# Loading half of one V unit of layer two by seven row-strided transfers instead of as part of one whole transfer

## The chip, the core and the metric

The kernel runs on one core of one Trainium2 chip. The metric is the time of one execution on the device in microseconds (us). Three runs of the kernel before took 648.73, 648.85 and 649.52 us; their median is 648.85 us. One further execution was recorded by the hardware profiler; all durations below are from it.

## What is computed

Two layers, each an attention block over a cache and a small gated network, applied twice to four rows `x` (one new token for each of four sequences). Both passes read the same weights and caches.

```python
def _A_ref(x, k_cache, v_cache, wq, wo):          # x (4,1,512), caches (4,8,8192,128) bf16
    q = (x @ wq).reshape(B, 1, 32, 128)           # 32 query heads, 8 cache heads
    scores = einsum("bhqd,bhkd->bhqk", q, k) * Dh ** -0.5
    o = einsum("bhqk,bhkd->bhqd", softmax(scores), v)
    return o.reshape(B, 1, 4096) @ wo
def _B_ref(x, w_gate, w_up, w_down):              # F = 1792
    return (silu(x @ w_gate) * (x @ w_up)) @ w_down
x = x + _A_ref(_layernorm(x), ...)
x = x + _B_ref(_layernorm(x), ...)
x = x + _A_ref(_layernorm(x), ...)
x = x + _B_ref(_layernorm(x), ...)
```

K and V together are 128 MiB, and each layer reads nearly all of it, so the work is mostly transfers from HBM into the on-chip memory (SBUF, 128 partitions).

## The kernel before, in words

**Units.** K and V are cut into 16 units each: two cache heads of one sequence. A unit fills one slot of the tile `kvf`, 128 partitions with 32 KB each. Partition p holds 128 consecutive tokens of one of the two heads, so the row that goes to a partition is one contiguous stretch of 32 KB in HBM. A unit is used in eight column blocks of 4 KB per partition (`NB = 8`, `BW` elements each); half a unit is 16 KB per partition.

**What is done with a unit.** For a K unit VectorE transposes each block in place (`turn`, line 488), TensorE multiplies each with the query (`scores`, line 512), then come the maximum, the exponentials on ScalarE (line 559) and the turning of the probabilities (line 576). For a V unit TensorE multiplies the probabilities with it in four parts (`values`, line 643; the first two parts read the first half), and VectorE gathers the result (lines 689 and 693). At the end of a layer the heads are mixed and projected (lines 724 to 784), and `ffn` runs the gated network (lines 876 and 897, with the weights loaded into a slot that has come free).

**Slots and loads.** There are four slots and a fifth (`QS`), and about 273 MB pass through them. All loads are issued by the SyncE queue (SP), in one order written out beforehand: the list `cmds` (lines 346 to 364). Layer two takes its units in the order 15, 14, 13, 12, 0 to 11; `loads` interleaves K and V, and `placed` deals them to the slots of a ring and cuts some into pieces (`half`, `ends`). A load enters the program when the column blocks it overwrites have been used: `freed` marks blocks as free and calls `pump`, which appends the next loads of the list as long as their blocks are free. On the chip the SP instruction then waits for the semaphore of the engine that used the block last (TensorE, for the units below). Because all five slots are kept full, SP is about three units ahead: a load is issued 30 to 40 us before it has landed.

**The unit of the change** is V of unit 5, the tenth in layer two's order (`V(1, us[9])`; "V9" below). It goes into slot 0 after K of unit 4 has been used there. In the profile SP issues it at 490.23 us, between K of the eleventh unit (472.97 us, "K10") and the next K ("K11", 492.40 us).

**Completion.** A transfer adds 16 to its semaphore when it has landed; the 16 DMA engines of the core share it. `load` (line 424) issues exactly one transfer for each entry of `cmds`.

Of the kernel before, what the change touches and what calls it, by code (L numbers as in the profile page):

```python
# [103 lines left out]
def bass_interleave_layers__gqa_block_cached__swiglu_ffn__decode_kernel(  # L104
# [18 lines left out]
    P = 128  # L123
# [6 lines left out]
    NB = 8  # L130
# [14 lines left out]
    with ExitStack() as es:  # L145
# [3 lines left out]
        BW = TB * Dh  # L149
# [6 lines left out]
        kv = kvf[:, 0:(NSLOT + 1) * SL].rearrange("p (s w) -> p s w", s=NSLOT + 1)  # L156
# [126 lines left out]
        T = _Sync(engines, prog)  # L283
# [35 lines left out]
        def pair_gb(u):  # L319
            return u // B, u % B  # L320

        order = [list(range(NP)), [NP - 1, NP - 2, NP - 3, NP - 4] + list(range(NP - 4))]
# [3 lines left out]
        V = lambda L, u: ("V", L, u)  # L326

        def loads(L, first):
            us = order[L]
            seq = []  # L330
            for i in range(first, NP - 1):
                seq += [K(L, us[i]), V(L, us[i - 1])]
            seq.insert(len(seq) - 1, K(L, us[NP - 1]))
            return seq[:-2] + [seq[-2], seq[-1], V(L, us[NP - 2]), V(L, us[NP - 1])]

        ends = lambda it, s: [(it, s, 0, QH), (it, s, QH, NB - 1), (it, s, NB - 1, NB)]
        half = lambda it, s: [(it, s, q, q + NB // 2) for q in range(0, NB, NB // 2)]

        def placed(seq, ring, parts):
            out = []  # L340
            for i, it in enumerate(seq):
                s = ring[i % len(ring)]
                out += parts[i](it, s) if i in parts else [(it, s, 0, NB)]
            return out

        us = order[0]
        seq = [K(0, us[0])] + loads(0, 1)
        assert len(seq) == 2 * NP
        cmds = placed(seq, (0, 1, 2, 3), {len(seq) - 1: ends})
# [6 lines left out]
        us = order[1]  # L356
        s = W_SLOT[0]
        cmds += [(K(1, us[1]), s, 0, 3), (K(1, us[1]), s, 3, 4), (K(1, us[1]), s, 4, NB)]
        cmds += [(K(1, us[2]), QS, 0, NB // 2), (K(1, us[2]), QS, NB // 2, NB - 2)]
        seq = loads(1, 3)  # L360
        ring = (0, 1, 3, QS, 2)
        cmds += placed(seq, ring, {0: half, 1: half, len(seq) - 1: ends})
        assert W_SLOT[1] == ring[len(seq) % len(ring)]
        cmds += [(("W", 1), W_SLOT[1], 0, NB), (("W+", 1), W_SLOT[1], NB, NB + 1)]

# [39 lines left out]
        def pump():  # L405
            while issued[0] < len(cmds):
                it, s, a, b = cmds[issued[0]]
                if it[0] == "wo":
                    load_weight(*it)
                else:  # L410
                    need = {(s, q) for q in range(a, b)}
                    if not need <= free:
                        return
                    free.difference_update(need)
                    if it[0] in ("W", "W+"):
                        load_weight(it[0], it[1], s)
                    else:
                        slot_of[it] = s
                        load(it, a, b, sem_s[s] if b - a == NB else part_sem())
                issued[0] += 1  # L420

        q_gone = set()

        def load(it, a, b, sm):
            kind, L, u = it
            s = slot_of[it]
            gp, bt = pair_gb(u)
            src = (A_k_cache if kind == "K" else A_v_cache)[bt, 2 * gp:2 * gp + 2, :, :].rearrange(
                "h (p t) d -> (h p) (t d)", t=TT)
            over = WQ if s == QS and not q_gone else []  # L430
            q_gone.update(over)
            T.dma("sp", kv[:, s, a * BW:b * BW], src[:, a * BW:b * BW], sm,
                  writes=[f"s{s}.{q}" for q in range(a, b)] + over)

        def freed(s, a, b):
            free.update((s, q) for q in range(a, b))
# [492 lines left out]
        for L in range(2):  # L929
            us = order[L]  # L930
# [61 lines left out]
```

## Time and profile before

| what | value |
|---|---|
| median of three runs | 648.85 us |
| the profiled execution's own time | 648.29 us |
| its span, first to last instruction | 646.50 us |
| bytes moved, mean rate over the span | 273.37 MB, 423 GB/s |
| V9 issued / landed | 490.23 / 525.17 us |
| last V pieces landed | 628.73, 632.46, 633.73 us |
| last weight piece (`w_down`) landed | 643.81 us |
| output issued | 644.94 us |

The profile's page lists busy time of each engine (PE is TensorE's matmul, PEld its weight loads, DVE VectorE, ACT ScalarE, POOL GpSimd, SP SyncE), then digits for 40 slices of the span (9 is 90% busy or more), the DMA queues, and the chain of work that ended last: from the last instruction back, each time to what released it. Besides these views the trace keeps, for every transfer, the times at which its semaphore was raised by each DMA engine (the landing records), and, for every DMA packet, its start, length and size (the packet records). Packet records do not name their engine, but on one engine a packet starts within a few nanoseconds of the end of the one before it, so the 16 series of packets can be followed from start to end.

### The profile page before, as it was taken

To read this page: it belongs to the slowest core of one execution; us is meant where nothing else is said; L and a number is where in the kernel's file an instruction comes from. 1 tells how busy PE (TensorE), PEld (TensorE's weight loads), DVE (VectorE), ACT (ScalarE), POOL (GpSimd) and SP (SyncE) were. 2 spreads that over 40 slices of the span, in tenths; PEclk is the share of its full clock that TensorE was granted. 3 is DMA by queue.
4 is the path that set the end of the run, shared out by engine and by line. 5 is a ranking of instruction groups with operands and counts; after the bars stand their busy time and mean duration, and the time that the engine had idled before them with its cause. 6 is when DMAs were issued, how large, how long until landed. Compare 5 with 4: busy or idle time off the path is not lost.

```text
span 646.5 us, 7503 instructions
## 1 busy us (share of the span) xinstructions
PE 425.6 (66%) x3128; PEld 173.1 (27%) x3128; DVE 430.1 (67%) x706; ACT 41.2 (6%) x117; POOL 11.1 (2%) x43
## 2 busy tenths in 40 slices
PE   2574466556766755767757987777665576657878
PEld 2221122212322212222226332222222222222225
DVE  1585467566776666777852878888766677766953
ACT  1000000000000000001010010000000000000110
POOL 0000000000000000000000000000000000000000
PEclk9996896789787999878985799999878997789977
DMA  9999999999999999999999999999999999999996
GB/s 363 445 423 416 442 429 430 426 435 433 426 430 435 430 425 436 435 422 436 434 407 409 396 435 434 434 429 423 442 427 426 433 438 424 431 440 423 430 417 268
DMA packets 14129, 273.37 MB, mean 423 GB/s; under 512 B 1416, under 2 KB 1424, under 8 KB 5264
## 3 DMA queue, kind: packets, MB, share of 16 engines
q1 hardware_dynamic: 14096, 272.91, 99.0%
q8 instruction: 24, 0.39, 0.2%
q14 instruction: 9, 0.07, 0.0%
HBM read 272.90 MB, written 0.00 MB: 422 GB/s over the span
## 4 chain that ended last, share of the span: by engine, by line
DMA 61%; DVE 26%; PE 9%; issue 3%; SPq 0%; ACT 0%; DVEq 0%
DMA kvf<-in_A_k_cache_dram 49%; DVE kvf L488 20%; DMA kvf<-in_A_v_cache_dram 10%; PE ps L512 3%; DVE pT L576 3%; PE ps L643 2%; DMA kvf<-in_B_w_down_dram 2%; DVE pb L693 2%; PE ps L839 1%; DVE pb L689 0%; PE ps L876 0%; DVE scr L703 0%; DVE kvf L452 0%; PE ps L759 0%; SPq L93 0%
## 5 line engine op out<-in xcount | busy, mean ns | idle before, releaser
L512 PE MATMUL ps<-kvf,zq 128*128 128x512 bf16 x1024 | 298.0, 426 | 181.1 <-DVE kvf L488 174.3
L488 DVE STREAM_TRANSPOSE kvf<-kvf 128x1024 f32<-128x1024 f32 x246 | 289.8, 1219 | 108.6 <-DMA kvf<-in_A_k_cache_dram 107.7
L512 PEld LDWEIGHTS ps<-kvf,zq 128*128 128x128 bf16 x1024 | 90.6, 105 | 350.9 <-DVE kvf L488 257.8
L643 PE MATMUL ps<-kvf,pT 128*32 128x512 bf16 x960 | 66.7, 400 | 1.4 <-DVE pT L576 0.8
L559 ACT ACTIVATE pb<-ps,tiny 128x512 bf16<-128x512 f32 x32 | 22.0, 688 | 531.8 <-DVE tiny L557 495.2
L576 DVE STREAM_TRANSPOSE pT<-pb 64x512 bf16<-64x512 bf16 x60 | 41.2, 687 | 3.1 <-ACT pb L559 2.0
L518 DVE TENSOR_REDUCE tiny<-ps 128x1 f32<-128x512 f32 x32 | 22.0, 687 | 31.6 <-PE ps L512 31.6
L693 DVE SCALAR_TENSOR_TENSOR pb<-ps,tiny,pb 128x128 f32<-128x128 f32 x104 | 36.5, 351 | 5.1 <-PE ps L643 1.3
L643 PEld LDWEIGHTS ps<-kvf,pT 128*32 128x32 bf16 x960 | 20.8, 98 | 31.9 <-issue 15.7
L698 PEld LDWEIGHTS ps<-sel,pb 128*128 128x128 f32 x64 | 15.4, 258 | 21.3 <-DVE pb L693 14.0
L502 POOL TENSOR_TENSOR zq<-scr,tiny 128x64 bf16<-128x64 bf16 x30 | 9.0, 300 | 564.8 <-PE ps L512 564.8
L526 DVE TENSOR_REDUCE mrm<-ps 1x8 f32<-1x128 f32 x32 | 8.8, 275 | 14.2 <-PE ps L523 14.2
L698 PE MATMUL ps<-sel,pb 128*128 128x8 f32 x64 | 12.7, 272 | 8.1 <-DVE pb L693 8.1
L549 PEld LDWEIGHTS ps<-mrm,tiny 128*128 128x128 f32 x60 | 12.0, 205 | 8.6 <-DVE scr L703 3.2
L759 PE MATMUL ps<-wo_sb,scr 128*4 128x512 bf16 x48 | 11.0, 379 | 1.5 <-DVE scr L728 1.5
L689 DVE TENSOR_SCALAR pb<-ps,tiny 128x128 f32<-128x128 f32 x32 | 10.1, 315 | 2.6 <-PE ps L643 2.6
L549 PE MATMUL ps<-mrm,tiny 128*128 128x16 f32 x60 | 9.3, 231 | 3.1 <-ACT mrm L561 3.1
L839 PE MATMUL ps<-xn,kvf 128*128 128x4 bf16 x256 | 7.6, 166 | 3.8 <-DMA kvf<-in_A_wq_dram 3.0
L561 ACT ACTIVATE mrm<-head,tiny 128x8 f32<-128x8 f32 x32 | 9.6, 301 | 1.0
L523 PE MATMUL ps<-identf,tiny 128*1 128x128 f32 x32 | 8.6, 270 | 0.2 <-DVE tiny L518 0.2
L839 PEld LDWEIGHTS ps<-xn,kvf 128*128 128x128 bf16 x256 | 7.6, 106 | 4.0 <-DMA kvf<-in_A_wq_dram 3.1
L876 PE MATMUL ps<-xn,kvf 128*128 128x4 bf16 x224 | 7.3, 169 | 1.8 <-DMA kvf<-in_B_w_up_dram 1.4
(83 smaller groups left out, 113.9 us busy)
## 6 DMA issues: line engine op xcount, KB each, us to landing
kvf<-in_A_k_cache_dram SPq DMA_DIRECT2D x28, 4096.0 KB, 30.8
kvf<-in_A_v_cache_dram SPq DMA_DIRECT2D x27, 4096.0 KB, 32.9
kvf<-in_A_v_cache_dram SPq DMA_DIRECT2D x4, 2048.0 KB, 20.0
kvf<-in_A_k_cache_dram SPq DMA_DIRECT2D x4, 2048.0 KB, 10.0
kvf<-in_A_wq_dram SPq DMA_DIRECT2D x2, 2048.0 KB, 9.8
wo_sb<-in_A_wo_dram SPq DMA_DIRECT2D x4, 1024.0 KB, 40.6
kvf<-in_B_w_gate_dram SPq DMA_DIRECT2D x2, 1792.0 KB, 24.5
kvf<-in_A_v_cache_dram SPq DMA_DIRECT2D x2, 1536.0 KB, 34.8
```

The costliest lines, as they stand in the source:

```text
L488: T.op("dve", lambda e: e.transpose(w, w), reads=[f"s{s}.{q}"], writes=[f"s{s}.{q}"])
L512: T.op("pe", lambda e: e.matmul(bank(bk)[:, 0:SW], lhsT=zq[:, z0:z0 + P], rhs=w[:, :, c // 2, :, c % 2], start=(q == 0 and c == 0), stop=( ...
L518: T.op("dve", lambda e: e.tensor_reduce(mx[:], bank(bk)[:, 0:SW], AX.X, ALU.max), reads=[f"pb{bk}"], writes=["mx"])
L549: T.op("pe", lambda e: e.matmul(at, lhsT=ones, rhs=mrm[:, i * H2:(i + 2) * H2], start=True, stop=True), reads=[f"m8{i}", "rsm", "onesf"], ...
L559: T.op("act", lambda e: e.activation(pb[:], bank(bk)[:, 0:SW], ACTF.Exp, bias=nm, accum_out=rs), reads=[f"pb{bk}", "nm"], writes=PB + ["rs"])
L576: T.op("dve", lambda e: e.transpose(dst, pb[hp]), reads=["pb", "row"], writes=[name])
L643: T.op("pe", lambda e: e.matmul(bank(k)[j * QB:(j + 1) * QB, q0 * Dh:q1 * Dh], lhsT=p_t[:, t, h, :], rhs=v[:, q0:q1, t, :], start=((last o ...
L689: T.op("dve", lambda e: e.tensor_scalar(into, o, own[:, q:q + 1], None, op0=ALU.mult), reads=[f"pb{k}", "own"], writes=["row"] if last els ...
L693: T.op("dve", lambda e: e.scalar_tensor_tensor(into, o, own[:, q:q + 1], into, op0=ALU.mult, op1=ALU.add), reads=[f"pb{k}", "own", iname], ...
L698: T.op("pe", lambda e: e.matmul(at, lhsT=into, rhs=sel[:], start=True, stop=True), reads=[iname, "sel"], writes=[name])
L759: T.op("pe", lambda e: e.matmul(bank(OUTB)[0:B, 0:D], lhsT=oT[:, h, :], rhs=wo_sb[:, h, :], start=(gp == groups[L][0] and r == 0), stop=(g ...
L839: T.op("pe", lambda e: e.matmul(at[:, h * B:(h + 1) * B], lhsT=wq_sb[:, kt, h * Dh:(h + 1) * Dh], rhs=xn[:, kt * B:(kt + 1) * B], start=(k ...
```

## The change

The list of loads cuts V9 into two halves, and the first half (columns 0 to 3 of 8, 16 KB in each partition) is issued as seven transfers over strided partitions: the 64 odd ones; the 32 that leave 2 when divided by 4; the 16 that leave 4 when divided by 8; and then four transfers of four partitions, 0, 32, 64, 96, and the same shifted by 8, 16 and 24. The seven share one semaphore, the second half has another. The wait for the slot is made once, ahead of the seven.

```diff
         seq = loads(1, 3)
         ring = (0, 1, 3, QS, 2)
-        cmds += placed(seq, ring, {0: half, 1: half, len(seq) - 1: ends})
+        cut = lambda it, s: [(it, s, 0, 4), (it, s, 4, NB)]
+        cmds += placed(seq, ring, {0: half, 1: half, seq.index(V(1, us[9])): cut, len(seq) - 1: ends})
...
+        uneven = (V(1, order[1][9]), 0)
+
         def load(it, a, b, sm):
...
-            T.dma("sp", kv[:, s, a * BW:b * BW], src[:, a * BW:b * BW], sm,
-                  writes=[f"s{s}.{q}" for q in range(a, b)] + over)
+            names = [f"s{s}.{q}" for q in range(a, b)] + over
+            rows = [slice(0, P)]
+            if (it, a) == uneven:
+                rows = [slice(i, P, m) for i, m in ((1, 2), (2, 4), (4, 8), (0, 32), (8, 32), (16, 32), (24, 32))]
+                T.wait_res("sp", writes=names)
+            for r in rows[:-1]:
+                T.dma("sp", kv[r, s, a * BW:b * BW], src[r, a * BW:b * BW], sm)
+            T.dma("sp", kv[rows[-1], s, a * BW:b * BW], src[rows[-1], a * BW:b * BW], sm, writes=names)
```

In the program that is built, the one SP entry of V9 becomes eight: 64, 32, 16 and four times 4 rows, and 128 rows for the second half. The order of the instructions of the other engines is the same.

## Prediction

> **What bounds the kernel now.** I began with the page: its span, the slices, and the DMA queues.
>
> ```profile
> span 646.5 us, 7503 instructions
> ...
> DMA  9999999999999999999999999999999999999996
> ...
> q1 hardware_dynamic: 14096, 272.91, 99.0%
> q8 instruction: 24, 0.39, 0.2%
> q14 instruction: 9, 0.07, 0.0%
> ```
>
> All 40 slices of the DMA row but the last are at 9, and the kernel's own loads (q1) fill 99.0% of the span of all 16 DMA engines. Queues 8 and 14 are instruction fetches: 24 of 16 KB and a few of 8 KB, which pass through the same engines. The busy time by stretch says the same of layer two: DMA share 1.00 and 1.01 up to 588 us, while TensorE and VectorE work two thirds of the time.
>
> ```profile
> 372.00:484.00 112.00, 80.70 (x510) 29.91 (x509) 86.34 (x135) 7.35 (x22) 2.10 (x7) 0.95 1.00 431
> 484.00:588.00 104.00, 66.13 (x393) 24.51 (x391) 71.75 (x108) 6.41 (x18) 1.80 (x6) 0.87 1.01 432
> 588.00:634.00 46.00, 35.20 (x241) 13.03 (x233) 32.13 (x60) 4.30 (x13) 0.79 (x2) 0.89 0.99 422
> ```
>
> Next the chain that ended last, in order of time.
>
> ```profile
> 472.97 42.49 DMA kvf<-in_A_k_cache_dram
> ...
> 588.37 40.36 DMA kvf<-in_A_v_cache_dram
> 628.73 0.04 issue
> 628.77 1.90 PE ps L643 x16
> ...
> 642.61 1.67 PE ps L897 x53
> 644.28 0.27 DVE pb L960
> ```
>
> It runs through long waits for transfers up to 628.73 us, then through the tail of the kernel. In the tail TensorE still waits for transfers: for the last two V pieces (landed 632.46 and 633.73 us, used at 632.50 and 633.78) and for the last weight piece, in the timeline of the end:
>
> ```profile
> 642.52 1.72 PE L897 MATMUL ps<-kvf,pb 128*4 128x128 bf16 x56
> 643.85 0.10 PEld L897 LDWEIGHTS ps<-kvf,pb 128*4 128x4 bf16 x8 [0.17 <-DMA kvf<-in_B_w_down_dram]
> ```
>
> So the end is the stream of transfers plus a fixed 2.7 us (643.81 to 646.50). What counts is when the **latest** DMA engine finishes, since a transfer has landed only when all its engines have. The landing records show how unequal they are: the first and last engine of V9 land 3.00 us apart (522.17 and 525.17), those of the last whole V unit 4.51 us apart (619.31 and 623.82), those of the last weight piece 4.33 us apart. Sorted, the engines' lags at that last V unit are 0, 0.13, 0.23, 0.70, 1.36, 1.42, 1.55, 1.69, then a step to 2.40, five from 2.77 to 2.92, 3.97 and 4.51 us. The packet records say why: each 16 KB instruction fetch puts the engine it falls on back by about 1.5 us. Eight engines are hit in turn, every eighth fetch the same one; after 370 us the other eight are spared. The spared are the first eight of the list.
>
> **The change, part by part.** *Rows per engine.* A whole transfer of 128 rows gives each engine 8 rows. The landing records show 16 raises for such a transfer, but for the one load of four rows (`x`, 1 KB each) four raises by engines and one more: four rows use four engines, one row each, and in the packet records four series hold one 1 KB packet each. I read the change by this: 64, 32 and 16 rows give every engine 4 + 2 + 1 = 7 rows, and the four transfers of four rows give 4 more to the same four engines. Twelve engines then carry 7 rows instead of 8 in this half, four carry 11. That all four-row transfers take the engines of `x` is my reading; the only other such load, the output, comes after a pause across which the series cannot be followed.
>
> *Price of a row.* Four half units in a row (issued 363.87 to 375.98 us) land at 374.51, 379.42, 384.30 and 389.21: 4.90 us for 8 rows of 16 KB, 0.612 a row. The six whole units that land from 515.47 to 573.75 us come every 9.71 us. A completion costs an engine one 4-byte packet of 9 ns in the packet records; I take 0.01 us.
> - Twelve engines: 7 x 0.612 + 3 x 0.01 + 4.90 (second half) = 9.21 us against 9.71: **0.50 us gained**.
> - Four engines: 11 x 0.612 + 7 x 0.01 + 4.90 = 11.70 us: **1.99 us lost**.
>
> *Which four.* Followed through the packet series from the 1 KB packets at 7.6 to 7.9 us, the four that loaded `x` are not among the eight hit by the 16 KB fetches up to 263 us; two of the four are followed clearly, two pass close to others. If so, their lag at the last V unit is at most 1.69, and 1.69 + 1.99 = 3.68 us, less than the 4.51 - 0.50 = 4.01 us of the latest. The latest engine gives 0.50 us and no other takes its place; the margin is 0.33 us. From there all remaining loads end 0.50 us earlier.
>
> *Is the 0.50 us passed on?* The loads behind V9 are queued long before, so every later landing moves by it. In the tail the V pieces, and the weight piece that ends last, are waited for by TensorE within 0.04 us of landing; the work between (633.78 to 642.52) follows from a landing as well and moves with it. So the whole is on the path: 0.50 us.
>
> *SP.* Seven issues more, 0.33 us each and 0.37 to 0.51 apart (606.80, 607.23, 607.74): up to 3.6 us. The first seven wait for the first four blocks of the K unit in slot 0 instead of all eight. In PE's timeline that unit's matmuls run from 477.92 us, the fourth block's end near 484 and the eighth's at 490.15; so the seven are out by 488, and the second half goes at 490.23 as V9 does now. Queued behind them on SP is K11 (492.40). Cover: at 484 us K10's load still has 31 us to go (landing 515.47). Without it each late issue would cost what it is late. I count nothing. Ten loads stood issued and not landed at 327 us, now twelve at 492; if the queue took no more, SP would stall a little inside the same cover.
>
> *Waits.* TensorE waits for V9 on two semaphores instead of one, once 0.05 us, in an engine with a third of its time free: nothing. The next load into the slot waits for both: landed long before.
>
> *Strided rows.* No transfer before has partitions in strides, so this cost is bounded. Below: zero, since a row of 16 KB takes 0.61 us in all loads. Above: each row at half the rate, 7 x 0.61 = 4.3 us on all engines. Nearest row: the four `x` packets go to partitions 0 to 3, two of them run at the same time (7.768 to 7.816 us), and all four take 46 ns; they do not slow each other. They are small, so I keep both ends and take zero.
>
> A rule against this: the Trainium skill, "SBUF — State Buffer", section "Door 1: The DMA port swizzle", says that groups of four partitions share a DMA port, 32 apart the same one. By it an engine that takes partitions 1, 3, 5, 7 changes port midway and meets another engine there, as far as ports are the limit; by it the sum could be the +3.8 us of the second rival. No run so far shows it.
>
> Sum: -0.50 us. On the profiled execution 648.29 - 0.50 = 647.8 us; it lies 0.56 us under the median, which gives 648.85 - 0.50 = **648.3 us** (0.08% less, within the 0.2%, or 1.3 us, that a measurement of this kernel can tell from no change).
>
> **Rivals.**
> 1. *The four engines are late ones.* For: two series are not certain. Against: the count above. From a lag of 4.01 - 1.99 = 2.02 us on they become the latest: with one of the group near 2.9 the end moves by 2.9 + 1.99 - 4.51 = +0.4, with the very latest by +2.0. 649.2 to 650.9 us.
> 2. *Slower: strided rows share ports.* Place: the seven transfers; price 0.61 us a row at half rate. It eats the gain from 0.07 us a row on (0.50 / 7), and shows as over 0.2% from 0.26 a row on (1.8 / 7). All seven rows: +4.3 - 0.5 = +3.8, 652.6 us; half of them, +1.6, 650.5 us. For: partitions never taken in this order before. Against: the `x` packets.
> 3. *It does not do what it says.* If the four-row transfers are spread over all 16 engines, each has 8 rows as now and pays some completions: +0.1, 648.9 us. Against: five raises for `x` instead of 16.
> 4. *More than 0.5 us.* A tail that answers more than one to one, down to 647.5 us. Nothing in the views shows where from; a gain over 0.61 us, one row, has no place in the sum.
>
> **How the numbers follow.** Forecast 0.62 (its own range 647.9 to 648.8, the scatter of the runs shown); rival 1 0.12; rival 2 0.14; rival 3 0.08; rival 4 0.04. The range 647.9 to 650.1 holds the forecast, rival 3 and most of rival 1, and leaves out most of rivals 2 and 4. Slower by over 0.2%: rival 2 and the worst of rival 1, 0.16. Faster by over 0.2%: 0.02. Within: 0.82.
>
> **What would show it.** In the profile after: 64 more semaphore packets and 128 more data packets on q1; the landing records of K11 and later 0.50 us earlier; first-to-last spreads 0.5 us smaller or led by other engines; the 2.7 us after the last weight piece as now. If the landing of the seven comes several us late, rival 2; if later spreads grow, rival 1; if nothing moves, rival 3. The forecast is wrong too if the fetches fall on other engines in other executions.

## The result, and the profile after

Six runs of the changed kernel took 654.02 to 656.21 us, median **655.22 us**; six of the kernel before 648.61 to 649.52, median 648.97. The ratio is 1.0096 (95% interval 1.0084 to 1.0107): 6.25 us slower, where 0.5 us less was forecast and 650.1 was the end of the range. The profiled execution took 654.25 us. One of the five executions of e10 below took 1940.22 us and is left out of its ratio.

From the page of the changed kernel, the span, the DMA digits, the rate by slice and the DMA queues:

```profile
span 652.5 us, 7511 instructions
...
DMA  9999999999999999999999999999999999999995
GB/s 368 433 425 420 440 431 428 429 434 429 430 432 429 432 431 434 431 430 430 426 411 401 416 437 429 436 425 435 428 431 432 353 406 436 427 434 431 428 415 207
...
q1 hardware_dynamic: 14288, 272.91, 98.7%
q8 instruction: 24, 0.39, 0.2%
q14 instruction: 9, 0.07, 0.0%
```

The bytes and the instruction fetches are those of before, q1 has 192 packets more (14,096 before), and the DMA digits are again all 9. By them nothing has changed. The rate row has the loss in two slices of 16.3 us: the 32nd and 33rd, 353 and 406 GB/s, from 506 to 538 us, around the landing of V9. Finer stretches show how deep it is. The next two answers are the busy times by stretch of the kernel before and then of the changed one, around the landing of V9; the last three columns are the granted TensorE clock, the share of time in which the DMA engines were busy, and GB/s.

```profile
509.00:515.00 6.00, 2.75 (x36) 0.84 (x34) 0.97 (x2) 0.00 (x0) 0.30 (x1) 1.00 1.01 434
515.00:521.00 6.00, 4.00 (x13) 1.67 (x14) 5.40 (x8) 0.00 (x0) 0.00 (x0) 0.72 1.01 431
521.00:527.00 6.00, 4.76 (x21) 1.60 (x19) 5.90 (x11) 1.08 (x3) 0.00 (x0) 1.00 0.96 415
527.00:533.00 6.00, 3.19 (x37) 1.05 (x37) 1.90 (x3) 0.00 (x0) 0.30 (x1) 1.00 0.99 426
```

```profile
509.00:515.00 6.00, 2.92 (x37) 0.90 (x35) 0.97 (x2) 0.00 (x0) 0.30 (x1) 1.00 0.96 410
515.00:521.00 6.00, 4.04 (x11) 1.74 (x12) 5.23 (x8) 0.00 (x0) 0.00 (x0) 0.56 1.09 287
521.00:527.00 6.00, 5.54 (x22) 2.15 (x20) 5.90 (x11) 1.08 (x3) 0.00 (x0) 0.87 0.97 322
527.00:533.00 6.00, 3.27 (x37) 1.05 (x37) 2.10 (x3) 0.00 (x0) 0.30 (x1) 1.00 1.03 442
```

From 515 to 527 us the busy share stays near 1 while the rate falls from 430 to about 300 GB/s: a packet that is held up counts as busy, so only bytes per time tell. The packet records say the same. Of the 256 packets of 16 KB of V9, 81 took over 1000 ns instead of 612, on all 16 engines, between 515.80 and 526.94 us; summed, 3.68 us more per engine. The 64 odd rows before them ran at 611 to 622 ns.

The landing records give the second part. K10 landed at 515.64 us (515.47 before), so everything up to there is as before. V9's first engine landed at 525.21 (522.17 before, +3.0), its last at 531.68 (525.17, +6.5); the spread from first to last grew from 3.0 to 6.5 us and stayed above 6 in the units behind. So some 3 us came to all engines and another 3 to one engine. K11 landed at 541.39 (534.90), the last weight piece at 649.79 (643.81). The chain and the end of the timeline show the delay passed on. The chain's wait for K11 is 48.84 us from issue to landing, against 42.50 before (492.40 to 534.90):

```profile
492.55 48.84 DMA kvf<-in_A_k_cache_dram
...
648.48 1.80 PE ps L906 x54
```

```profile
649.83 0.10 PEld L906 LDWEIGHTS ps<-kvf,pb 128*4 128x4 bf16 x8 [0.28 <-DMA kvf<-in_B_w_down_dram]
...
650.91 0.30 SPq L971 DMA_DIRECT2D out_dram<-pb  x1
```

The last product still waits for the last weight piece, and 2.7 us remain after its landing (649.79 to 652.5), as before.

### The profile page after: what moved, and what is told of

The parts are those of the page before. It is cut to its first block, busy times and chain, and to the rows that moved or that the text cites. A ratio compares the mean times of both kernels' runs of the same rounds, so it can differ in the third digit from the quotient of the medians.

```text
span 652.5 us, 7511 instructions
## 1 busy us (share of the span) xinstructions
PE 424.1 (65%) x3128; PEld 173.3 (27%) x3128; DVE 430.2 (66%) x706; ACT 41.2 (6%) x117; POOL 11.1 (2%) x43
## 4 chain that ended last, share of the span: by engine, by line
DMA 56%; DVE 30%; PE 9%; issue 3%; ACT 0%; SPq 0%; POOL 0%; ACTq 0%; POOLq 0%; DVEq 0%
DMA kvf<-in_A_k_cache_dram 50%; DVE kvf L497 22%; DMA kvf<-in_A_v_cache_dram 4%; PE ps L521 4%; DVE pT L585 3%; DVE pb L702 3%; PE ps L652 2%; DMA kvf<-in_B_w_down_dram 2%; DVE pb L698 1%; PE ps L848 1%; PE ps L885 0%; DVE scr L712 0%; DVE ps L464 0%; DVE tiny L527 0%; DVE kvf L461 0%
```

## Experiments

Most of these kernels change only the line `rows = [...]` of the changed kernel, so that its list is the whole diff. e5 and e6 also read from a second list, and e8 and e16 add transfers to the kernel before; of these four the main lines are shown. Each is compared with the kernel before on the same chip (648.36 to 648.48 us in the four groups). "Excess" is the time above 0.612 us of V9's 16 KB packets, summed and divided by 16 engines.

**Is it the cut, the unequal rows, the order or the strides?** The first group: the cut alone; equal rows with 16-row transfers; neighbouring partitions; and four-row transfers eight apart instead of 32.

```diff
e1  rows = [slice(0, P)]
e2  rows = [slice(i, P, m) for i, m in ((1, 2), (2, 4), (4, 8), (0, 8))]
e3  rows = [slice(i, i + n) for i, n in ((0, 64), (64, 32), (96, 16), (112, 4), (116, 4), (120, 4), (124, 4))]
e4  rows = [slice(i, P, m) for i, m in ((1, 2), (2, 4), (4, 8))] + [slice(i, i + 32, 8) for i in (0, 32, 64, 96)]
```

> V9 in two halves of 128 rows each, no seven transfers. All theories: the cut is not the cause; 649.0 us, within 0.3 us of before, packets of the half at 0.61 us. If it is over 650, the cut itself (its second semaphore or the earlier issue) has a share.

Measured 648.51 us, ratio 1.0001 [0.9991, 1.0010]; excess 0.07 us. The cut costs nothing.

> First half as 64, 32, 16 and 16 strided rows: 8 rows for each engine, no four-row transfers. Theory P (strided partitions contend, from the 16-row transfer on, for whatever they share): slower, two rows of eight at half rate or worse, 650 to 653 us, with packets of over 1 us. Theory F (the four-row transfers alone slow all engines): as before, 649.0 us. Theory I (only the unequal load of 11 rows): as before, 649.0.

Measured 651.80 us, 1.0051 [1.0036, 1.0066]; excess 2.49 us. The spread between the engines has not grown (2.2 us in V9's second half and behind it, 3.0 before). Every engine has its 8 rows here, so 3.4 us come from the way the rows are cut, without any inequality.

> The same seven sizes over neighbouring rows: 0 to 63, 64 to 95, 96 to 111, then 112 to 127 in fours. Theory P (stride): packets back at 0.61 us and only the unequal load left, 648.5 to 651. Theory F: slow packets as in the changed kernel, 654 to 656. If neighbouring rows contend more than strided ones (each small transfer then lies in few groups of partitions), over 656.

Measured 661.27 us, 1.0200 [1.0183, 1.0217]; median packet 1170 ns, excess 8.58 us, slow from 512.0 us on, so from the first transfer. The same numbers of rows in neighbouring partitions cost twice as much.

> 64, 32 and 16 rows as in the changed kernel; the four-row transfers take partitions 8 apart (0, 8, 16, 24 and so on) instead of 32 apart. If the four-row transfers contend because two of their four partitions lie 32 apart, 650 to 652 us with fewer slow packets; if it is the 16-row transfer or the unequal load, as the changed kernel, 654 to 656.

Measured 654.40 us, 1.0099 [1.0084, 1.0114]: as the changed kernel. How far the four rows stand apart hardly matters.

**HBM or SBUF?** A transfer's rows are strided on both sides. e5 keeps the SBUF partitions of the changed kernel and reads neighbouring rows of HBM; e6 does the reverse (partitions of e3, strided rows of HBM). e7 is 64 odd and 64 even partitions. e8 puts three tiny loads of one, two and four rows (8, 12 and 10 bytes) ahead of four V units of the kernel before; their sizes make them findable in the packet records, so that they tell when the engines that serve them get there.

```diff
e5, e6  T.dma("sp", kv[r, s, a * BW:b * BW], src[f, a * BW:b * BW], sm)   # f: the other order
e7      rows = [slice(i, P, 2) for i in (1, 0)]
e8      for n, w in ((1, 4), (2, 6), (4, 5)):
            T.dma("sp", mark[0:n, at_m[0]:at_m[0] + w], src[0:n, 0:w], m, writes=[f"mark{at_m[0]}"])
            at_m[0] += w
```

> The seven transfers with the strided partitions of the changed kernel, but each reads neighbouring rows from HBM, as in e3; so half a unit of V stands in other partitions than its own, and the output is not the reference's. If the contention lies on the SBUF side (which partitions are written together): as the changed kernel, 654 to 656 us, slow packets from about 515.8 us on, 3.7 us lost per engine. If it lies on the HBM side (which rows are read together): as e3, 660 to 662 us, 8.6 us lost per engine.

> The reverse of e5: neighbouring partitions are written as in e3, rows are read from HBM with the strides of the changed kernel; half a unit of V stands in other partitions than its own, and the output is not the reference's. SBUF side: as e3, 660 to 662 us, slow packets from 512 us on. HBM side: as the changed kernel, 654 to 656 us.

e5 654.72 us, 1.0096 [1.0075, 1.0116]; e6 661.42 us, 1.0199 [1.0179, 1.0219], two executions each. e5 is the changed kernel again, e6 is e3 again. The SBUF partitions decide, the rows of HBM do not.

> First half as two transfers of 64 rows, the odd partitions and the even ones: 8 rows for each engine. The 64-row transfer of the changed kernel ran at full rate in its packet records, so the theory that only the sparser strides (16 rows, every eighth partition) contend gives no change, 648.4 us within 0.5. If any stride contends once it is the last one out, over 650 us.

Measured 648.46 us, 1.0004 [0.9994, 1.0013], median packet 613 ns. Stride 2 is free.

> The kernel before, with three tiny transfers of one, two and four rows (8, 12 and 10 bytes a row) ahead of four of the loads, V9's among them; they go to a spare tile that nothing reads. Nothing is left out; time as before, within 0.5 us. The odd sizes show in the packet records which series belong to the engines that serve four-row transfers. Theory of the prediction: all four among the eight earliest at V9, lag under 1.8 us. Theory that the unequal load costs: at least one of the four among the late ones, near 2.9 us.

Measured 648.66 us, 1.0001 [0.9991, 1.0011]. The four packets of 10 bytes start at 512.42, 512.44, 513.03 and **515.53** us ahead of V9, and at 609.52, 609.56, 610.16 and 613.65 ahead of a later V unit. Of the four engines three are early and one is 3 to 4 us late, in the kernel before already. The loads of one and two rows ran on early ones.

**Which sets are slow?** Four more cuts of the half. With 112 rows and then fours or pairs the rows of each engine are 7 and 11 (or 15); with 32 and 16 rows they are 8 everywhere.

```diff
e9   rows = [slice(16, P)] + [slice(i, i + 4) for i in (0, 4, 8, 12)]
e10  rows = [slice(16, P)] + [slice(i, i + 2) for i in range(0, 16, 2)]
e11  rows = [slice(i, P, 4) for i in range(4)]
e12  rows = [slice(i, P, 8) for i in range(8)]
```

> The half of V9 goes as one transfer of partitions 16 to 127 (7 rows for each engine) and then four transfers of four neighbouring partitions (0-3, 4-7, 8-11, 12-15). The load on the engines is exactly that of the changed kernel: 7 rows, 11 on four engines. Theory U (unequal load on its own: one of the four engines is a late one, about 3 us behind the first even in the kernel before): the late engine carries 4 rows at 0.612 us more, -0.50 + about 2.5 us against the cut without strides, so 650.0 to 651.0 us, and in later units one engine stands about 5.5 us behind the first. Rival P (all of the +6 us comes from slow rows in narrow sets of partitions): 112 neighbouring partitions run at full speed, only the four engines work in partitions 0 to 15, so 648.4 us within 0.3, or, if four engines in 16 neighbouring partitions slow all others as well, over 652.

> As the kernel with 112 rows and four times four, but the last 16 rows go as eight transfers of two neighbouring partitions. By the markers two-row transfers use two engines, and both of them are early ones, about 3 us ahead of the late group here and about 4 at the end. They carry 15 rows, 14 others 7. If the lead of an early engine absorbs what is put on it: +7 x 0.612 = 4.3 us on the two, less a lead of 3 to 4, so 648.0 to 649.5 us, faster than the kernel with four-row transfers although the load is more unequal. If every engine counts alike (no early and late ones): 648.4 + 4.3 = 652.7 us.

e9 658.31 us, 1.0164 [1.0147, 1.0181]; e10 660.67 us, 1.0189 [1.0172, 1.0206]. Both miss what was expected of the unequal load: the 112 rows were slow from 512.5 us on, before any of the fours or pairs. So they do not tell the load by itself, and they ask why 112 neighbouring partitions are slow when 128 are not. In the units behind them the spread is 5.4 and about 7.6 us, and the rate of whole loads is 432 GB/s again.

> The half of V9 as four transfers of 32 partitions, each four apart (0 mod 4, 1 mod 4, 2 mod 4, 3 mod 4): every engine has 2 + 2 + 2 + 2 rows, 8 as before. If only sets of 16 partitions or fewer are slow: 648.4 us within 0.4 and packets of 16 KB at a median of 0.61 us. If the 32 rows of the changed kernel were slow by themselves: 650 us or more.

> The half of V9 as eight transfers of 16 partitions, each eight apart: every engine has one row of each, 8 as before. If a set of 16 partitions eight apart is slow for as long as it lasts (1.45 us for a row against 0.61, as in the kernel with 64, 32, 16 and 16 rows): 8 x 0.84 = 6.7 us more, 655 us. If it is slow only while engines that lead and engines that lag stand in different transfers, or if neighbouring transfers overlap and fill each other's gaps: 649 to 652 us. If slowness came from the change between transfers alone, 648.5.

e11 648.41 us, 1.0001 [0.9992, 1.0010]; e12 656.21 us, 1.0116 [1.0102, 1.0130]. The stretches of e11 and then of e12:

```profile
515.00:521.00 6.00, 3.88 (x11) 1.74 (x12) 5.08 (x8) 0.00 (x0) 0.00 (x0) 0.50 1.02 429
521.00:527.00 6.00, 5.11 (x22) 1.72 (x20) 5.90 (x10) 1.08 (x3) 0.00 (x0) 0.99 1.09 470
```

```profile
509.00:515.00 6.00, 3.17 (x37) 1.03 (x37) 0.97 (x2) 0.00 (x0) 0.30 (x1) 1.00 1.02 320
515.00:521.00 6.00, 0.30 (x1) 0.13 (x2) 1.60 (x2) 0.00 (x0) 0.00 (x0) 0.53 0.97 205
521.00:527.00 6.00, 6.00 (x21) 2.70 (x20) 5.86 (x13) 0.28 (x1) 0.00 (x0) 0.61 1.01 218
527.00:533.00 6.00, 4.09 (x21) 1.23 (x22) 4.80 (x6) 0.79 (x3) 0.00 (x0) 1.00 1.02 412
```

Thirty-two rows four apart run at 429 GB/s and more, 16 rows eight apart at 205 to 218, half of it. The fall begins before 515 us, when the last engines are still in K10, and K10's own 32 KB packets then take up to 2.62 us there; their median is 1.22. One engine that reaches a slow transfer holds up engines in another one.

**Number of ports, or who meets whom?** The last group tells two readings apart. In S the number of ports that a transfer's partitions reach sets its rate. In H each engine keeps to its own partitions in whole loads and in the free strides, and is slowed where the rows are dealt out so that two engines meet in one group. e16 takes the unequal load alone: the kernel before, with four loads of four rows that go from HBM to a spare HBM tensor and never touch SBUF (their result is not used).

```diff
e13  rows = [slice(0, 64), slice(64, P)]
e14  rows = [slice(32, 96), slice(0, 32), slice(96, P)]
e15  rows = [slice(0, 96), slice(96, P)]
e16  for i in range(0, 16, 4):
         T.dma("sp", spare[i:i + 4, :], src[i:i + 4, 0:NB // 2 * BW], m, writes=[f"spare{i}"])
```

> The half of V9 as partitions 0 to 63 and then 64 to 127; every engine has 4 + 4 rows, 8 as before. Theory S (what counts is how many of the 16 ports of the swizzle table in the Trainium skill, 'SBUF — State Buffer', 'Door 1: The DMA port swizzle', a transfer's partitions reach: 0 to 63 reach 8, so half the rate): 8 rows at half rate, +4.9 us, 653.3 us, up to 655 with what spills to the neighbouring loads. If only transfers with fewer than 64 rows were slow: 648.5 us.

> The half of V9 as partitions 32 to 95, then 0 to 31, then 96 to 127: 4 + 2 + 2 rows for every engine. Theory S: 32 to 95 reach all 16 ports of that table and run at full speed, the two others reach 8 each: 4 rows at half rate, +2.45 us, 650.9 us within 0.8. If neighbouring partitions short of a whole load are slow whatever ports they reach: 8 rows, as for 0 to 63 and 64 to 127, 653 to 655 us.

> The half of V9 as partitions 0 to 95 and then 96 to 127: 6 + 2 rows for every engine. Theory S: 0 to 95 reach all 16 ports, only the last 32 rows are slow: 2 rows at half rate, +1.2 us, 649.6 us. Theory H (in whole loads, in the odd 64 and in every fourth 32 each engine keeps to the same few partitions, so no two engines meet; 96 or 112 rows are dealt out in another way, engines meet in the same group of partitions, and engines behind them too): all 8 rows slow, +4.9 us or more, 653 to 657 us, as the kernel with 112 rows was slow from its first rows on.

e13 656.52 us, 1.0125 [1.0111, 1.0139]; e14 653.39 us, 1.0077 [1.0063, 1.0091]; e15 657.06 us, 1.0131 [1.0111, 1.0151]. The stretches of e13, then of e14 and then of e15:

```profile
509.00:515.00 6.00, 3.20 (x37) 1.05 (x37) 1.07 (x3) 0.00 (x0) 0.30 (x1) 0.97 1.05 325
515.00:521.00 6.00, 0.00 (x0) 0.00 (x0) 0.94 (x1) 0.00 (x0) 0.00 (x0) 0.50 0.94 197
```

```profile
509.00:515.00 6.00, 3.19 (x37) 1.05 (x37) 1.31 (x3) 0.00 (x0) 0.30 (x1) 1.00 0.99 407
515.00:521.00 6.00, 2.19 (x6) 0.79 (x7) 3.39 (x6) 0.00 (x0) 0.00 (x0) 0.50 1.02 216
```

```profile
509.00:515.00 6.00, 3.20 (x37) 1.05 (x37) 1.09 (x3) 0.00 (x0) 0.30 (x1) 1.00 1.02 330
515.00:521.00 6.00, 0.00 (x0) 0.00 (x0) 0.52 (x1) 0.00 (x0) 0.00 (x0) 0.58 1.14 194
521.00:527.00 6.00, 5.22 (x17) 2.39 (x18) 5.89 (x9) 0.00 (x0) 0.00 (x0) 0.57 0.90 178
```

In e14 partitions 32 to 95 run at full speed: K10's first engine lands at 512.63 us, that of the 64 rows at 515.11, 4 rows in 2.48 us. Only the two sets of 32 behind them are slow, and cost more than S gave them (4.9 us instead of 2.45). In e13 partitions 0 to 63, also 64 neighbours, take 5.04 us (512.50 to 517.54), twice as long. That agrees with the Trainium skill, "SBUF — State Buffer", section "Door 1: The DMA port swizzle", by whose table 32 to 95 reach all 16 ports and 0 to 63 only 8. But in e15 partitions 0 to 95 reach all ports too and run at 178 to 194 GB/s: **S falls**. A weaker S, in which the port with the most rows sets the pace, falls as well: by that table 64 of the 96 rows lie on 8 ports, 8 rows each, which at 0.612 us a row would take 4.9 us, an estimate of 320 GB/s. H expected 653 to 657, and e15 stands at the upper end. The Trainium skill, "DMA: Bandwidth & Descriptors", section "The descriptor swizzle", says that in a 128-partition transfer each engine writes just one port. Whole loads at 432 GB/s with any spread between the engines (2.2 us in e2, 7.6 in e10) agree with it. Which engine writes which row is in no record here, so H is supported and not seen. Nor does it say by itself why 32 to 95 are free and 0 to 63 are not. If neighbouring rows were dealt out in equal runs, four to an engine, that table would give just this; but the odd 64 dealt out in such runs would meet as well, as the prediction has it, and they are free (e7). So which sets are slow is shown, and how the rows are dealt out stays open.

> The kernel before, with four more transfers of four rows of 16 KB ahead of V9 that go from HBM to a spare tensor in HBM and never touch SBUF: they put 4 rows each on the four engines that serve four-row transfers, and their result is not used. Theory U (one of the four is a late engine): its later landings go back by 4 times what such a row takes, +2.45 us if it is 0.612, so about 650.8 us and a first-to-last spread of about 5.8 us instead of 3.4; the other three, early ones, show no more than their lead. If all four were early, as predicted: at most +0.3, 648.4 to 648.7 us, spread as before.

Measured 650.69 us, 1.0039 [1.0024, 1.0053]. The stretches of e16:

```profile
515.00:521.00 6.00, 4.57 (x13) 1.95 (x14) 5.77 (x8) 0.00 (x0) 0.00 (x0) 0.50 1.02 440
521.00:527.00 6.00, 4.56 (x21) 1.68 (x19) 5.90 (x11) 1.08 (x3) 0.00 (x0) 1.00 1.01 437
```

The rate never falls, and still the end is 2.21 us later. The 16 packets take 611 to 615 ns; three of the four engines are through theirs by 514.6 us, the fourth works on its four from 514.64 to 517.1. V9's spread is 5.56 us instead of 3.0 (3.6 in e8 and 4.1 in e1, which put no rows on it). Four rows on one late engine go through to the end almost whole (2.21 of 2.45), and the same rows on three early engines add nothing that is seen: in V9 all engines but one have landed by 524.78 us, the last at 527.25.

## Why the prediction was wrong, by its own steps

- **What bounds the kernel**: right. The stream of transfers plus 2.7 us; what V9 lost arrived at the end (V9 +6.5 us, K11 +6.5, last weight piece +6.0, median +6.25).
- **Rows per engine**: right as to the numbers. The four four-row transfers raise their semaphore by four engines each and by the sequencer (486.86, 487.42, 487.96 and 488.50 us), and q1 has the 192 packets more that were expected.
- **Price of a row**: right for undisturbed rows (611 to 622 ns for the 64 odd ones); the 0.50 us saved on twelve engines was never seen, since all were held up.
- **"Which four"**: failed for one engine. From series that I could follow only in part I concluded that all four are among the early engines. In the changed kernel they stand 0, 0.06, 0.24 and 2.90 us behind the first at K10, and e8 finds the same in the kernel before. Rival 1 was true, at 2.90, and its +0.4 for that lag was too small, because this engine falls further back: 4.1 us behind the first in e8 at 613.65 us, close to the latest. With 4.1 the rival's own sum gives 4.1 + 1.99 - 4.51 = +1.6. e16 sizes it: 2.21 us for four rows more, so about 1.7 for the three more of the change.
- **"Strided rows"**: the larger failure. Zero was taken by the nearest row, the four 1 KB packets of `x`. They were too few and too small to show it: 4 of 16 engines, 46 ns. The upper end, half the rate, was the right price, and the place of rival 2 ("the seven transfers") was too wide. The 64 and 32 rows are free (e7, e11); a 16-row transfer runs at half rate (e12), and its neighbours with it. With equal rows this alone costs 3.4 us (e2).
- **The sum as measured**: 3.4 (e2) + 1.7 (from e16) = 5.1 of 6.25 us. The intervals of the two leave about 1.0 and 0.7 us open, so the missing 1.1 us may be scatter. Nor are the two independent: the last four landings of the seven transfers (524.06, 525.11, 526.16 and 527.07 us), which fit the late engine's last rows, stand about 1.0 us apart instead of 0.612; 4 x 0.39 = 1.6 us would cover the rest, but partly repeats what e2 holds. How the last 1.1 us divides was not tried by itself.
- **SP and the waits**: right. The seven were issued from 483.99 to 487.58 us, K11 at 492.55 (492.40 before), with K10 landing at 515.64: the cover held.
- **Rivals 3 and 4**: out. Each four-row transfer was raised by four engines and not by 16, and nothing was gained.

The rivals had the causes, each with its own price, but both happened at once, which none of the cases held; rival 2's 3.8 and rival 1's 2.0 together, 5.8, would have been near the 6.25. No cut that was run is faster than the kernel before.

## What to carry to other kernels

When all DMA engines are full, cut a load only into sets of partitions that have been measured as free. Here whole loads, every second or every fourth partition over the whole height, and 32 to 95 (as the first transfer of e14) were free, while sixteen partitions eight apart, halves such as 0 to 63, and 96 or 112 neighbours ran at about half rate or less and slowed the load ahead of them too. That this goes by which engines meet was argued and not seen. Read GB/s in short stretches beside the busy share, because a held-up transfer looks busy. Before giving a few engines more rows, find out when just these engines arrive: a tiny transfer with a size of its own marks them in the packet records at no cost (1.0001).

## What the runs showed of the hardware that was not expected

- The rate falls for all engines and not just for those in the slow transfer. In e12 it is 320 GB/s from 509 to 515 us, when the last engines were still in K10's whole rows: K10 landed at 519.38 us there instead of 515.5. The Trainium skill, "DMA: Bandwidth & Descriptors", section "Back-pressure in remote DMA", tells of a full SBUF port that holds up the engines on the same path, for transfers between cores; these are loads from HBM, so the numbers here show only that something alike happens.
- 96 neighbouring partitions (e15, +8.6 us) cost as much as two sets of 64 (e13, +8.0) or 16 rows eight apart (e12, +7.8); the intervals overlap. A larger set of partitions was no better by its size alone.
- Lags between engines are kept to the end. What one late engine received in V9 at 515 to 532 us stands as a spread of over 6 us in the units behind it; whole loads give every engine the same, and no later load evened it out.
